# An mLSTM cell and a GELU layer on one core: 32-token products in the first chunk's values, and one batch of exponentials moved forward

## The chip, the cores and the metric

The kernel runs on one core of one Trainium2 chip. The metric is the time of one execution on the device in microseconds (us). A core has five engines with instruction streams of their own, each worked off in order: TensorE (PE in the profile; its weight loads are PEld), VectorE (DVE), ScalarE (ACT), GpSimd (POOL) and SyncE (SP), which here issues transfers. An instruction waits for others on semaphores.

## What is computed

The reference, cut to what matters. First a recurrent cell for each of 4 batches and 8 heads, over 768 tokens of width 40:

```python
for t in range(S):
    m_new = np.maximum(f_gate[:, :, t] + m, i_gate[:, :, t])
    f_stab = np.exp(f_gate[:, :, t] + m - m_new)
    i_stab = np.exp(i_gate[:, :, t] - m_new)
    m = m_new
    C = f_stab[:, :, None, None] * C + i_stab[:, :, None, None] * np.einsum('bhd,bhe->bhde', vt, kt)
    n = f_stab[:, :, None] * n + i_stab[:, :, None] * kt
    h_tilde = np.einsum('bhde,bhe->bhd', C, qt)
    denom = np.maximum(np.abs(np.einsum('bhd,bhd->bh', n, qt)[:, :, None]), 1.0)
    y[:, :, t] = 1.0 / (1.0 + np.exp(-o_gate[:, :, t])) * h_tilde / denom
```

Then the heads are laid side by side (3072 rows of 320) and go through two layers, `h = x @ w_in`, the exact GELU, `g @ w_out`, with a hidden width of 2048.

## The kernel before

The 768 tokens are six chunks of 128. Within a chunk the recurrence is written as products: scores of keys with queries, weighed by exponentials of the gates, times the values, and besides a contribution of the state that the chunks before have left. After the cell of a chunk its 512 rows (4 batches x 128 tokens) go through the two layers. The first chunk's up-projection takes part of its hidden rows as plain float32 products and part split in three parts that are added up; the later chunks take all of them in parts. In the input the layer weights are read as bit patterns and converted in pieces: ACT takes the two halves of a word apart (`conv_one`, lines 404 and 405, letter K of the order), DVE puts them together (`conv_two`, lines 416 and 419, letter J), and `fetch` (line 394) then loads a later piece into the buffer that has become free.

The order of the work is written out by hand, in strings of words that `play` (line 1019) works off one by one. A word is a letter and a batch number. `FRONT` (lines 26 to 31) holds the first chunk's cell in small letters, the second's in capitals, the conversions and the first chunk's two layers. All engines get their instructions in this order, and each keeps to it. The letters that the change and the prediction touch, for the second chunk and batch b:

- M: `mask`, line 474, on POOL: fills the upper triangle of the batch's tile W, which a transfer (`load_M`) has filled.
- W: `weights`, line 500, on ACT: eight exponentials, one per head, in place in W. For the first chunk (w) they are taken from PE's product pm.
- T: `turn`, lines 530 and 533: PE turns the batch's keys and queries into the bank pt, ACT copies them out as kT and qT.
- S: `scores`, lines 552 and 555: PE multiplies kT with qT, DVE multiplies the result into W.
- C: `carry`, lines 590 to 610: the state's part of the result and the state's update.
- V: `values`, line 656: PE multiplies W, now as the operand that is loaded, with the values, into the bank ph.
- Y and X: `finish` and `turn_y`, lines 685 to 718: the normalised output and its turned copy, whose high part x_hi ACT makes at line 718; DVE makes the rest at lines 727 and 728 (letter R).
- f2, f3: `first_pair`, lines 787 to 797: 36 products of the first chunk's up-projection in parts, and four GELUs on ACT.
- F: `first_down_steps`, line 888: the first chunk's down-projection; its last rows take split operands, whose middle part DVE makes at line 874.

In `values` a batch's eight heads go through the loop at line 655: in the first chunk each head's 128 tokens are two products of 64, in the second chunk four of 32. Each lands on its own partitions of ph:

```python
            for h in range(H):
                for r in halves if self.c == 0 else quarters:
                    nc.tensor.matmul(ph[r, h, :], Pm[:, h, r], vb[turn_of(n)][:, h, :], start=True, stop=True)
```

ACT keeps one set of function tables at a time. Where an exponential follows a GELU, or a GELU an exponential, the build places a load of the other set (ACT_TABLE_LOAD); copies and the conversions need none.

Of the kernel before, what the change touches and what calls it, by code (L numbers as in the profile page):

```python
# [25 lines left out]
FRONT = """  # L26
    O0 L0 k1 P0 E L1 L2 t0 P1 k7 K w0 g0 N s0 w1 O1 O3 D k4 t1 P2 w2 c0 v0 J y0 Q s1 L3 O2 K d w3 q t2 L4 P3 v1
    g1 c1 J y1 s2 K x0 t3 x1 v2 g2 O4 J B4 g3 c2 y2 s3 B5 K x2 K L5 J T0 K v3 A y3 M1 x3 c3 G0 M0 H O7 O6 O5 J
    J i5 u0 L6 u1 K W0 J W1 I4 A K S0 T1 C0 J i6 V0 i7 u2 G2 K U M2 L7 S1 J G1 K U i8 W2 J i9 C1 T2 K
    M3 f2 S2 V1 Y0 T3 J Y1 C2 e W3 K K K J S3 J C3 f3 K X0 J K R0 J K J V2 K Y2 J J K  # L30
    K V3 X1 J K r F J K (0 )0 F J K F K J F X2 G3 F J K F Y3 R1 J K F p + + + + J F J a10,2 b10,2 z10 a12 b12 F X3 z11 F a13,3 b13,3 z12 F z13 [1 F B8 z14 F B9 R2 z15 F R3 B10 B11 F a8 b8 a9 b9 F"""
CELL = "MWGVYXRKQDCSht"

# [23 lines left out]
def kernel(  # L57
# [95 lines left out]
    halves = (slice(0, R), slice(R, P))  # L153
    quarters = tuple(slice(R // 2 * n, R // 2 * (n + 1)) for n in range(4))
# [41 lines left out]
    def turn_of(n):  # L196

        return n % NLD if n < 2 * B else (n - 2 * B) % NQ
# [198 lines left out]
    def conv_one(i):  # L397

        if i < len(pieces):
            n = bits[i].shape[1]  # L400
            lo, hi = bits[i][:, :, 0], bits[i][:, :, 1]
            s = sig[i] = raw.tile([P, WP], F32, name="sig", tag="sig")[:, 0:n]
            p = pow2[i] = raw.tile([P, WP], U32, name="pow", tag="pow")[:, 0:n]
            nc.scalar.activation(out=s, in_=hi.bitcast(F32), func=AF.Copy, scale=2.0 ** -112)  # L404
            nc.scalar.activation(out=p, in_=lo, func=AF.Relu, scale=0.9 * 2.0 ** -29, bias=low_bits)
# [4 lines left out]
    def conv_two(i):  # L410

        if i < len(pieces):
            bits.pop(i)
            to = sig[i] if 4 < i < 10 else pieces[i][1]
            dst, s, p = to.bitcast(U32), (sig[i] if 4 < i < 10 else sig.pop(i)).bitcast(U32), pow2.pop(i)
            nc.vector.scalar_tensor_tensor(out=p, in0=s, scalar=3, in1=p, op0=OP.logical_shift_left, op1=OP.bitwise_or)  # L416
            if i >= 10:
                dst, s, p = in_pairs(dst), in_turns(s), in_turns(p)
            nc.vector.scalar_tensor_tensor(out=dst, in0=s, scalar=0x80000000, in1=p, op0=OP.bitwise_and, op1=OP.bitwise_or)  # L419
            if i != HELD:  # L420
                fetch(i + NB - (i > HELD))
# [8 lines left out]
    def unread(bank):  # L430
        for _ in range(idle[0]):
            nc.tensor.matmul(bank, ident, ident, start=True, stop=True, skip_group_check=True)
        idle[0] = 0
# [24 lines left out]
    class Cell:  # L458
# [190 lines left out]
        def values(self, b):  # L649
            n = self.c * B + b  # L650
            Pm = W.pop(n)
            ph = self.hs[b] = ps_h.tile([P, H, D1], F32, name="ph", tag="h")
            unread(ph.rearrange("p h d -> p (h d)")[:, 0:P])
            for h in range(H):
                for r in halves if self.c == 0 else quarters:
                    nc.tensor.matmul(ph[r, h, :], Pm[:, h, r], vb[turn_of(n)][:, h, :], start=True, stop=True)
            if self.c > 0:
                hs = self.hs[b] = self.far.pop(b)
                nc.vector.tensor_tensor(out=hs, in0=ph, in1=hs, op=OP.add)
# [172 lines left out]
    def first_up_steps(h):  # L832

        def step(k):
            ups.append((len(ups) + len(tags_next) % 2, (2 * k, 2 * k + 2, HT * h, HT * h + HT)))
            if len(ups) == 2:
                first_up()

        return [lambda k=k: step(k) for k in range(HF // 2)]
# [37 lines left out]
    def first_down_steps(g):  # L877
        po = []

        def row(n):  # L880

            if n == 0:
                po.extend(ps_mm.tile([P, DM], F32, name="po", tag="ab"[b // 2]) for b in range(B))
            xs, ws = ((g.row(n),), (w_row(n),)) if n not in first_parts_of else (first_parts_of[n], later.w_parts(n))
            steps = [(k, b) for k in range(len(xs)) for b in range(B)]
            for k, b in sorted(steps, key=lambda x: x[::-1]) if n == NF - 1 else steps:
                to, w = (po[b], ws[k]) if len(xs) == 1 else (in_pairs(po[b]), in_turns(ws[k]))
                nc.tensor.matmul(to, xs[k][:, b * L:(b + 1) * L], w, start=(n == 0 and k == 0),  # L888
                                 stop=(n == NF - 1 and k + 1 == len(xs)), skip_group_check=True)
                if n == NF - 1 and k + 1 == len(xs):  # L890
                    if b % 2 == 0:
                        o_sb = outp.tile([P, 2, DM], F32, name="o_sb", tag="o_sb")
                    nc.scalar.activation(out=o_sb[:, b % 2, :].rearrange("p (a i) -> p a i", a=2),
                                         in_=po[b].rearrange("p (i a) -> p a i", a=2), func=AF.Copy)
                    send(0, b, o_sb[:, b % 2, :])

        return [lambda n=n: row(n) for n in range(NF)]
# [128 lines left out]
    def in_turn(steps):  # L1026
        todo = list(steps)
        return lambda: todo.pop(0)() if todo else None
# [9 lines left out]
    def first_blocks():  # L1038
# [3 lines left out]
        for r in (32, 96):  # L1042
# [9 lines left out]
                 A=in_turn(first_up_steps(0)), U=in_turn(first_up_steps(1)), e=first_blocks, F=in_turn(first_down_steps(first_g)),  # L1052
                 K=in_turn(lambda i=i: conv_one(i) for i in n_pieces), H=products_begin,
                 J=in_turn(lambda i=i: conv_two(i) for i in n_pieces), Z=split_weight,
# [53 lines left out]
```

## Time and profile before

| | us |
|---|---|
| median of 3 runs | 438.06 |
| lowest and highest | 437.81, 439.68 |
| the profiled execution | 439.45 |
| its span in the profile | 437.7 |

The profile gives, for each engine, the busy time, and in a list by time each instruction or group of like instructions: start, length, engine, line, operation, the tile that is written and the tiles that are read, the shapes, the count, and in brackets how long the engine had been idle before and what ended that. The span runs from the first to the last instruction; the rest of an execution's time lies around it. Durations below come from this one execution.

### The profile page before, as it was taken

How to read it: one execution, taken by the hardware profiler on the slowest of the kernel's cores; microseconds unless marked ns; L12 is line 12 of the kernel's file. 1: busy time of each engine (PE TensorE's matmuls, PEld its weight loads, DVE VectorE, ACT ScalarE, POOL GpSimd, SP SyncE). 2: the span in 40 equal slices, each digit the busy share in tenths (PEclk: the TensorE clock that was granted, in tenths of full speed). 3: DMA queues.
4: the chain of work that ended last, by engine and by line, in shares of the span. 5: the costliest groups of instructions: out<-in, count | busy, mean ns of one | idle time of the engine just before them, and what ended most of it. 6: DMA issues, size and time to landing. Idle time of an engine off the chain costs nothing.

```text
span 437.7 us, 13034 instructions
## 1 busy us (share of the span) xinstructions
PE 429.5 (98%) x5344; PEld 376.6 (86%) x5344; DVE 295.6 (68%) x680; ACT 277.3 (63%) x595; POOL 50.0 (11%) x77
## 2 busy tenths in 40 slices
PE   9999999999999999999999999999999999999996
PEld 8778778877888898988898988898988889979986
DVE  7897777797888697737587737596746586533330
ACT  3989999965898985128776228795247715243441
POOL 3000212000530041030041030040010000000000
PEclk9999999999999999999999999999999999999999
DMA  7998996477791493563483564481561400010001
GB/s 153 198 211 228 196 247 164 124 197 197 210 184 56 88 191 63 108 172 63 65 179 69 107 165 69 94 157 32 108 157 18 61 1 1 18 45 1 1 1 60
DMA packets 162267, 48.81 MB, mean 112 GB/s; under 512 B 147776, under 2 KB 155232, under 8 KB 162208
## 3 DMA queue, kind: packets, MB, share of 16 engines
q1 hardware_dynamic: 161888, 47.65, 50.3%
q8 instruction: 42, 0.69, 0.7%
q10 hardware_dynamic: 320, 0.33, 0.2%
q14 instruction: 17, 0.14, 0.1%
HBM read 43.84 MB, written 9.37 MB: 122 GB/s over the span
## 4 chain that ended last, share of the span: by engine, by line
PE 73%; DVE 2%; ACT 2%; DMA 1%; issue 1%; ACTq 0%
PE po L991 31%; PE pu L966 24%; PE pu L977 7%; PE ps L568 3%; PE pf L621 2%; PE ph L674 1%; PE po L888 1%; PE po L674 1%; PE px L708 1%; DMA bits<-in_moe_w_out_dram 1%; PE pf L632 1%; ACT w_out_part L935 0%; DVE pow L416 0%; DVE w_out L419 0%; ACT sig L404 0%
## 5 line engine op out<-in xcount | busy, mean ns | idle before, releaser
L991 PE MATMUL po<-w_out_part,g_parts 128*128 128x320 f32 x960 | 140.7, 303 | 0.0
L991 PEld LDWEIGHTS po<-w_out_part,g_parts 128*128 128x128 f32 x960 | 131.6, 189 | 5.9 <-issue 4.6
L986 DVE TENSOR_TENSOR g_parts<-g_whole,g_parts 128x512 fp32r<-128x512 f32 x80 | 56.2, 702 | 57.8 <-ACT g_parts L985 55.7
L984 ACT ACTIVATE g_whole<-pu 128x512 f32<-128x512 f32 x80 | 47.2, 590 | 73.1 <-PE pu L977 62.6
L985 ACT ACTIVATE g_parts<-g_whole 128x512 fp32r<-128x512 f32 x80 | 50.5, 631 | 8.3 <-PE po L991 5.1
L474 POOL TENSOR_SCALAR_AFFINE_SELECT W<-W 128x1024 f32<-128x1024 f32 (+2 forms) x20 | 22.8, 1146 | 191.0 <-DMA W<-M_d 116.5
L500 ACT ACTIVATE W<-W,aT 128x128 f32<-128x128 f32 x128 | 38.7, 388 | 0.4 <-POOL W L474 0.2
L987 DVE CAST g_parts<-g_whole 128x512 fp32r<-128x512 f32 x80 | 36.3, 454 | 0.0
L699 ACT COPY far<-ob 128x128 f32<-128x128 f32 x16 | 4.6, 290 | 32.8 <-DVE ob L690 32.8
L966 PE MATMUL pu<-x_hi,w_in_hi 128*128 128x512 f32 x80 | 24.2, 384 | 0.0
L966 PE MATMUL pu<-x_hi,hi_first 128*128 128x512 f32 x80 | 23.9, 380 | 0.0
L966 PE MATMUL pu<-x_low,w_in 128*128 128x512 f32 x80 | 23.8, 379 | 0.0
L966 PE MATMUL pu<-x_rest,hi_first 128*128 128x512 f32 x80 | 23.8, 379 | 0.0
L966 PE MATMUL pu<-x_low,w_in_lo 128*128 128x512 f32 x80 | 23.8, 379 | 0.0
L966 PE MATMUL pu<-x_rest,w_in_hi 128*128 128x512 f32 x80 | 23.8, 379 | 0.0
L888 PE MATMUL po<-w_out,g 128*128 128x320 f32 x80 | 22.0, 432 | 0.0
L404 ACT ACTIVATE sig<-bits 128x320 f32<-128x320 f32 (+1 forms) x26 | 15.2, 585 | 10.6 <-issue 6.1
L574 DVE TENSOR_TENSOR W<-ps,W 128x256 f32<-128x256 f32 (+1 forms) x48 | 17.7, 413 | 4.2 <-PE ps L568 4.0
L888 PEld LDWEIGHTS po<-w_out,g 128*128 128x128 f32 x80 | 15.0, 190 | 5.9
L512 DVE STREAM_TRANSPOSE kT<-blocks 128x512 f32<-128x512 f32 x16 | 11.3, 709 | 12.0 <-DMA blocks<-kq_d 11.8
L639 DVE TENSOR_TENSOR far<-pf,gT 128x164 f32<-128x164 f32 x32 | 8.4, 319 | 14.7 <-PE pf L632 11.4
L1015 ACT ACTIVATE o_sb<-po 128x320 f32<-128x320 f32 x20 | 7.5, 442 | 16.7 <-PE po L991 16.7
(196 smaller groups left out, 788.3 us busy)
## 6 DMA issues: line engine op xcount, KB each, us to landing
W<-M_d SPq DMA_DIRECT2D x16, 512.0 KB, 6.6
bits<-in_moe_w_in_dram SPq DMA_DIRECT2D x20, 256.0 KB, 4.7
bits<-in_moe_w_out_dram SPq DMA_DIRECT2D x16, 320.0 KB, 4.8
blocks<-kq_d SPq DMA_DIRECT2D x32, 128.0 KB, 3.5
ob<-in_o_gate_dram SPq DMA_DIRECT2D x24, 160.0 KB, 4.3
out_dram<-o_sb SPq DMA_DIRECT2D x36, 80.0 KB, 2.0
wide<-M_d SPq DMA_DIRECT2D x4, 512.0 KB, 4.8
kq_d<-in_k_dram SPq DMA_DIRECT2D x6, 320.0 KB, 4.8
```

Source lines behind the costliest of these rows:

```text
L404: nc.scalar.activation(out=s, in_=hi.bitcast(F32), func=AF.Copy, scale=2.0 ** -112)
L474: nc.gpsimd.affine_select(out=x, in_=x, compare_op=OP.is_ge, fill=1.0e30, base=base, pattern=[[0, H], [1, x.shape[2]]], channel_multiplier=-1)
L500: nc.scalar.activation(out=W[n][:, h, :], in_=src, func=AF.Exp, scale=-1.0, bias=aT[:, self.c, r:r + 1])
L574: nc.vector.tensor_tensor(out=w[r, :, t], in0=ps[i][hip][r, :, t], in1=w[r, :, t], op=OP.mult)
L888: nc.tensor.matmul(to, xs[k][:, b * L:(b + 1) * L], w, start=(n == 0 and k == 0), stop=(n == NF - 1 and k + 1 == len(xs)), skip_group_chec ...
L966: nc.tensor.matmul(in_pairs(pus[i][e]), w3(at[k])[n][:, e, i * P:(i + 1) * P], in_turns(x3[n][:, k, :]), start=(n == 0 and k == 0), stop=F ...
L977: nc.tensor.matmul(in_pairs(pus[i][e]), w3(r)[n][h, p % 2, i * P:(i + 1) * P], in_turns(x3[n][h, NX, :]), start=False, stop=(n == 2), skip ...
L984: nc.scalar.activation(out=whole, in_=self.pus[n // 4][n % 4 // 2][n % 2], func=AF.Gelu)
L985: nc.scalar.activation(out=hi, in_=whole, func=AF.Copy, scale=PART)
L986: nc.vector.tensor_tensor(out=rest, in0=whole, in1=hi, op=OP.subtract)
L987: nc.vector.tensor_copy(out=low, in_=whole)
L991: nc.tensor.matmul(in_pairs(self.po[t]), x[:, t * L:(t + 1) * L], in_turns(w), start=(n == 0 and k == 0), stop=(n == NF - 1 and k == 2), s ...
```

## The change

Two things. In `values` the loop takes quarters of 32 tokens in the first chunk too. And in the written order the second chunk's fourth mask, M3, stands ahead of its old place by some words, and its fourth batch of exponentials, W3, directly behind T2 (the third batch's kT and qT) and so ahead of a conversion (K), the pair f2 and T3. In the order of the instructions this moves nothing on POOL, DVE and SP; on PE only the form of the values' products differs; on ACT the eight exponentials move up past one conversion, four GELUs and the two copies of T3, and two table loads are no longer placed.

```diff
-    J i5 u0 L6 u1 K W0 J W1 I4 A K S0 T1 C0 J i6 V0 i7 u2 G2 K U M2 L7 S1 J G1 K U i8 W2 J i9 C1 T2 K
-    M3 f2 S2 V1 Y0 T3 J Y1 C2 e W3 K K K J S3 J C3 f3 K X0 J K R0 J K J V2 K Y2 J J K
+    J i5 u0 L6 u1 K W0 J W1 I4 A K S0 T1 C0 J i6 V0 i7 u2 G2 K U M2 L7 S1 J G1 M3 K U i8 W2 J i9 C1 T2 W3 K
+    f2 S2 V1 Y0 T3 J Y1 C2 e K K K J S3 J C3 f3 K X0 J K R0 J K J V2 K Y2 J J K
...
-                for r in halves if self.c == 0 else quarters:
+                for r in quarters:
```

## The prediction

> **What bounds the kernel now.** I read the page first, then the waits of TensorE (PE), then the stretches ahead of the change, then the order of time on each engine.
>
> ```profile
> PE 429.5 (98%) x5344; PEld 376.6 (86%) x5344; DVE 295.6 (68%) x680; ACT 277.3 (63%) x595; POOL 50.0 (11%) x77
> ```
>
> PE is busy 98% of the span of 437.7 us, so nearly every microsecond that PE loses or gains is a microsecond of the kernel, unless a wait further on takes it up. The next view is the list of waits of PE alone between 33 and 126 us; its columns are the total, the count and the longest, in us.
>
> ```profile
> PE po L888 <- DVE g_part L874: 0.7, 2, 0.4
> PE ps L552 <- ACT qT L533: 0.4, 1, 0.4
> PE ph L656 <- DVE W L555: 0.3, 1, 0.3
> ```
>
> Three waits, 1.4 us in all, are everything that PE loses there. So a saving ahead of the waits at lines 656 and 552 only makes these longer, if the engines that end them keep their time; and a loss behind them can be taken up only by the 0.7 us at line 888. Which engine keeps that time is told by two rows of the stretches (their length, then the busy time of PE, PEld, DVE, ACT and POOL, then the granted clock, the share of the transfer engines, GB/s):
>
> ```profile
> 16.00:34.00 18.00, 16.59 (x266) 14.23 (x268) 15.03 (x41) 14.99 (x44) 0.00 (x0) 1.00 1.06 217
> 45.00:68.97 23.97, 23.30 (x260) 19.27 (x257) 17.25 (x28) 23.73 (x52) 6.43 (x6) 1.00 1.07 242
> ```
>
> From 45 to 68.97 us ScalarE (ACT) is busy 23.73 of 23.97 us: it has more to do than PE and has no hole. In the first chunk, 16 to 34 us, nobody is full (PE waits 1.41 us, ACT 3.01 us), but the transfer engines are (share 1.06). Now the order of time on ACT, on which the whole sum rests:
>
> ```profile
> 33.81 0.69 ACT L404 ACTIVATE sig<-bits 128x512 f32<-128x512 f32 x1 [1.60 <-DMA bits<-in_moe_w_in_dram]
> ...
> 55.66 0.62 ACT L533 COPY qT<-pt 128x512 f32<-128x512 f32 x1
> ...
> 68.49 0.57 ACT L533 COPY qT<-pt 128x512 f32<-128x512 f32 x1
> 68.97 0.62 ACT L404 ACTIVATE sig<-bits 128x320 f32<-128x320 f32 x1
> ...
> 70.19 1.28 ACT L797 ACT_TABLE_LOAD   x1
> 71.48 2.07 ACT L797 ACTIVATE g<-pu 128x512 f32<-128x512 f32 x4
> 73.52 0.59 ACT L533 COPY kT<-pt 128x512 f32<-128x512 f32 x1
> 74.12 0.59 ACT L533 COPY qT<-pt 128x512 f32<-128x512 f32 x1
> 74.72 1.28 ACT L500 ACT_TABLE_LOAD   x1
> 76.02 2.44 ACT L500 ACTIVATE W<-W,aT 128x128 f32<-128x128 f32 x8
> 78.37 0.57 ACT L404 ACTIVATE sig<-bits 128x320 f32<-128x320 f32 x1
> ...
> 81.96 1.28 ACT L797 ACT_TABLE_LOAD   x1
> 83.81 2.06 ACT L797 ACTIVATE g<-pu 128x512 f32<-128x512 f32 x4 [0.56 <-PE pu L793]
> 85.73 0.55 ACT L404 ACTIVATE sig<-bits 128x320 f32<-128x320 f32 x1
> ...
> 86.64 0.51 ACT L718 ACTIVATE x_hi<-px 128x384 fp32r<-128x384 f32 x1
> ```
>
> The reader is to see that ACT's dense stretch starts on a transfer at 33.81, and that the copies of kT and qT of the fourth batch (73.52, 74.12) end at 74.71. PE needs them here:
>
> ```profile
> 74.50 0.77 PE L595 MATMUL pf<-state,qT 128*64 128x82 f32 x16
> 75.20 1.16 PE L552 MATMUL ps<-qT,kT 64*128 64x128 f32 x16
> 76.29 0.67 PE L590 MATMUL pf<-vw,qk 128*64 128x41 f32 x16
> ...
> 77.48 1.99 PE L787 MATMUL pu<-first_x_hi,hi_first 128*128 128x512 f32 x8
> ...
> 84.35 0.44 PE L708 MATMUL px<-ident,ob 128*128 128x128 f32 x2
> ```
>
> The scores of the fourth batch (75.20) follow the products before them at once: qT was ready 75.20 - 74.71 = 0.49 us early. That is all the slack there is.
>
> **The exponentials moved.** The fourth batch's eight exponentials (line 500, 76.02) go from behind the fourth batch's kT and qT to behind the third's, that is to 68.97, ahead of a conversion (lines 404, 405), the load of the GELU table and four GELUs. Nothing new is issued; on GpSimd, VectorE and SyncE's queue the order stays. Two table loads fall away: at 68.97 the exponential's table is still in place, so the load at 74.72 goes, and with no exponential between the two groups of GELUs the load at 81.96 goes too, 2 x 1.28 = 2.56 us of ACT. The exponentials wait for the fourth batch's mask:
>
> ```profile
> 64.56 1.55 POOL L474 TENSOR_SCALAR_AFFINE_SELECT W<-W 128x1024 f32<-128x1024 f32 x1 [1.31 <-PE pt L530]
> ```
>
> It ends at 66.11, 2.86 us before 68.97: no wait is added there. But now the ready time of qT is put together anew, from the same rows, each step from its start to the start of the next: exponentials 78.37 - 76.02 = 2.35; conversion 70.19 - 68.97 = 1.22; table load 71.48 - 70.19 = 1.29; four GELUs 73.52 - 71.48 = 2.04; kT 68.97 - 68.49 = 0.48 (that spacing stands for kT as for qT, since both copies have their operand by then); qT 0.57. So qT ends at 68.97 + 2.35 + 1.22 + 1.29 + 2.04 + 0.48 + 0.57 = 76.92. The step from the end of that copy to PE's start is in a row quoted below: the second batch's copy ended at 55.66 + 0.62 = 56.28, its scores started at 56.34, 0.06 later. Scores then start at 76.98 and not at 75.20: **PE loses 1.78 us**. Behind the waiting scores stand, on PE, the fourth batch's carry (76.29) and the 36 products of the last up-projection pair (77.48 to 84.35); all start 1.78 later. Their banks are free by then (the four GELUs end 2.35 later, at 75.90, before 77.48 + 1.78).
>
> What the loads saved is worth: nothing. The load at 74.72 lay behind the copies that PE waits for. The load at 81.96 ended at 83.24, and the GELUs behind it waited until 83.81 for PE; PE now comes later. The exponentials themselves were in no hurry where they stood, since their reader on VectorE (DVE) came at 80.56, after they had ended at 78.46:
>
> ```profile
> 80.56 1.28 DVE L555 TENSOR_TENSOR W<-ps,W 128x512 f32<-128x512 f32 x2
> ```
>
> What is late next: the GELUs go from 83.81 to 85.59, behind them on ACT the conversion at 85.73 and the x_hi copy at 86.64, and from there the chain of work that ended last goes on without a hole:
>
> ```profile
> 87.18 0.56 DVE x_rest L727
> ...
> 113.88 6.24 PE po L888 x44
> ```
>
> Between these two rows it runs through DVE, ACT and one transfer of the output weights, and comes back to PE at 113.88, which is one of the two waits at line 888. So the chain that ends that wait begins with the very GELUs that are 1.78 late. Both PE (dense from 84.35) and the chain slip by the same amount, so I let the 0.7 us take up nothing. Full cover would be worth 0.7.
>
> **The values of the first chunk.** Each of four batches is 16 products of 64 columns, now 32 of 32 columns; the trace shows two records per product. It also shows the new form, in the second chunk:
>
> ```profile
> 18.58 1.11 PE L656 MATMUL ph<-vb,W 128*64 128x41 f32 x32
> 19.62 0.37 PE L276 MATMUL pg<-ident,ew 32*128 32x32 f32 x3
> ...
> 56.34 1.16 PE L552 MATMUL ps<-qT,kT 64*128 64x128 f32 x16 [0.36 <-ACT qT L533]
> ...
> 85.59 0.81 PE L656 MATMUL ph<-v,W 128*32 128x41 f32 x64
> 86.33 0.44 PE L708 MATMUL px<-ident,ob 128*128 128x128 f32 x2
> ```
>
> Old form: 19.62 - 18.58 = 1.04 us to the next work. New: 86.33 - 85.59 = 0.74. So 0.30 saved a batch, at most 1.2 us in all. The Trainium skill, TensorE: Matmul & The Clock Gate, section "Wait — 56ns, not 53.3ns?", speaks against the edit: starts never come closer than about 25 ns, and by that 64 records would take 1.6 us, 0.56 more than now. This trace differs: 0.74 us for 64 records is 12 ns each, since four column groups take turns, and the measurement decides.
>
> What it is worth at the end: the first of the four batches starts at 18.58 and all stand on PE ahead of the scores at 56.34. PE comes 1.2 us earlier to what follows and waits there, at line 656 for DVE and at 56.34 for ACT (0.36 now). ACT's time at 56.34 goes back without a hole to 33.81, where it waited 1.60 us for a transfer of input weights. The queue that issued it:
>
> ```profile
> 28.61 1.95 SPq L394 DMA_DIRECT2D bits<-in_moe_w_in_dram x4
> ```
>
> By the code that load's buffer is fresh, so PE need not release it; the loads ahead of it need only early work of the first batch. I therefore take 0 for this edit. The bounds: 0 if the transfers keep their time; if the queue does wait for PE, the two batches ahead of 28.61 give up to 0.6; all four cannot give more than 1.2 by PE alone.
>
> **The sum.** +1.78 (scores late) + 0 (loads, exponentials) + 0 (values) = +1.78 us. For the profiled execution that is 437.7 + 1.78 = 439.5 of span and 439.45 + 1.78 = 441.2 of time. That execution was 1.39 above the median of the runs, 438.06; on the median the forecast is 438.06 + 1.78 = **439.8 us**. A measurement of this kernel can tell about 0.5%, or 2.2 us, from no change, so this is a small loss that would count as the same.
>
> **The rivals.**
> (a) The early gain is handed on in part: ACT's dense stretch starts 0.5 sooner, 439.3. For it: the saved time does lie ahead of 33.81, and the wait view puts some of the queue's waits down to PE there. Against it: transfer share 1.06.
> (b) The waits at line 888 take up the 0.7: 439.1. For it: the conversions at 78.37 start about 1.5 us earlier (they follow the start of qT, 76.92 - 0.57 = 76.35, by 0.48), so some weights are fetched sooner. Against it: the chain above.
> (c) Faster. ACT has 3.01 us of waits between 16 and 34. If the shorter values let more than 1.78 of them go, no scores wait is left and the kernel gains; with all 3.01 gone it ends at 438.06 + 1.78 - 3.01 = 436.8. Against it: 1.60 of the 3.01 is the transfer at 33.81, and PE saves only 1.2.
> (d) Slower: PE's clock falls in the new hole. The hole lies between small products, and the start of the kernel shows what a slow clock costs:
>
> ```profile
> 3.82 2.08 PE L250 MATMUL cold<-w_out 128*128 128x128 f32 x8
> ...
> 9.24 1.73 PE L250 MATMUL cold<-w_out 128*128 128x128 f32 x14
> ```
>
> 260 ns each at 3.82 against 124 at 9.24, the granted clock notwithstanding, so about twice as slow; slow work lasted from about 1.1 to 5.8 us, 4.8 us. The same after the hole would lose half of that, 2.4 us, off the products from 77.48: 439.8 + 2.4 = 442.2. It decides if a hole of 1.78 us is enough; the holes of up to 0.4 us above were not. The same page of the Trainium skill, section "What's actually happening", gives about 3.4 us idle as the point where the clock drops, which no row here shows; by that the hole is too short, and where it did drop, half of 3.4, 1.7 us, would be lost.
>
> **How the numbers follow.** The forecast has 0.55, (a) 0.15, (b) 0.08, (c) 0.07, (d) 0.15. The forecast, (a) and (b) lie between 439.1 and 439.8; with 0.7 either side for the spread of the runs (437.81 to 439.68) that is 438.4 to 440.5. Half of (d), with a shorter slow stretch, brings the top to 441.5; left out are (c) and the rest of (d). Over 440.25 lies (d) and about a fifth of the forecast: slower 0.27. Under 435.9 lies only an end beyond (c)'s: faster 0.03. The same 0.70.
>
> **What would show it right or wrong.** A wait of PE for ACT's qT at the fourth batch's scores, near 1.7 us, with the exponentials at about 69.0, one table load between 65 and 100 us behind them, and GELUs at about 85.6: right. If that wait is absent, the step of ACT's rows was wrong. If ACT's conversion near 33.8 comes sooner, (a) or (c). If the two waits at line 888 are gone while the chain before them kept its time, (b). If the 36 products take more than 6.9 us, (d). If the values of the first chunk still take about 1.0 us a batch, the edit doesn't do what it says, at no cost to the sum.

## The result and the profile after

| | before | after |
|---|---|---|
| median of 20 executions each, us | 438.4 | 439.8 |
| lowest and highest | 437.38, 440.1 | 438.78, 441.87 |
| the profiled execution, its span | 439.45, 437.7 | 440.12, 438.3 |

The ratio is 1.0029, 95% interval 1.0019 to 1.0039: on 438.4 us a loss of 1.3 us, 0.8 to 1.7. The forecast was 439.8, from 438.06, the median of the first three executions, plus 1.78. That it meets the measured time to the tenth is luck: with 20 executions the kernel before stands at 438.4, 0.34 higher, and the loss is smaller than 1.78 by about as much.

The page of the kernel after, its line of busy times:

```profile
PE 428.4 (98%) x5472; PEld 375.2 (86%) x5472; DVE 296.1 (68%) x680; ACT 273.7 (62%) x593; POOL 50.4 (11%) x77
```

PE's busy time fell by 1.1 us and ACT's by 3.6, with two instructions fewer on ACT (the table loads), and yet the span grew by 0.6: busy time saved is not time gained. PE's waits of the kernel after, 33 to 126 us, tell where it went:

```profile
PE ps L552 <- ACT qT L533: 1.8, 2, 1.4
PE po L888 <- DVE g_part L874: 0.8, 2, 0.4
PE ph L656 <- DVE W L555: 0.2, 1, 0.2
```

The wait for qT was 0.4 us in one place; now it is 1.8 in two, with a new one of 1.4. Its place, in PE's order of time of the kernel after:

```profile
18.46 0.82 PE L656 MATMUL ph<-vb,W 128*32 128x41 f32 x64
19.21 0.37 PE L276 MATMUL pg<-ident,ew 32*128 32x32 f32 x3
...
34.29 3.72 PE L818 MATMUL pu<-first_x,w_in 128*128 128x256 f32 x16
...
55.44 1.16 PE L552 MATMUL ps<-qT,kT 64*128 64x128 f32 x16 [0.35 <-ACT qT L533]
...
75.78 1.16 PE L552 MATMUL ps<-qT,kT 64*128 64x128 f32 x16 [1.40 <-ACT qT L533]
...
78.06 1.99 PE L787 MATMUL pu<-first_x_hi,hi_first 128*128 128x512 f32 x8
...
84.93 0.44 PE L708 MATMUL px<-ident,ob 128*128 128x128 f32 x2
```

The fourth batch's scores (75.78) are what waits. From 78.06 to 84.93 the 36 products take 6.87 us, as before (77.48 to 84.35). The values of a batch take 19.21 - 18.46 = 0.75 us. And on ACT, after:

```profile
68.07 2.45 ACT L500 ACTIVATE W<-W,aT 128x128 f32<-128x128 f32 x8
70.41 0.48 ACT L404 ACTIVATE sig<-bits 128x320 f32<-128x320 f32 x1
...
71.40 1.28 ACT L797 ACT_TABLE_LOAD   x1
72.69 2.06 ACT L797 ACTIVATE g<-pu 128x512 f32<-128x512 f32 x4
74.62 0.62 ACT L533 COPY kT<-pt 128x512 f32<-128x512 f32 x1
75.08 0.65 ACT L533 COPY qT<-pt 128x512 f32<-128x512 f32 x1
...
79.74 0.63 ACT L404 ACTIVATE sig<-bits 128x320 f32<-128x320 f32 x1 [2.28 <-issue]
...
84.39 2.06 ACT L797 ACTIVATE g<-pu 128x512 f32<-128x512 f32 x4 [3.42 <-PE pu L793]
```

The order is the one foretold: exponentials, conversion, one load, GELUs, then the fourth batch's kT and qT. The second group of GELUs waits 3.42 us for PE, where it waited 0.56, and a conversion at 79.74 starts after 2.28 us of idle time that was not there before. What ACT no longer does between the copies and these GELUs, the exponentials and two loads, has turned into idle time.

**Where executions differ.** The profiled execution of before lies 1.05 us above its median (439.45 against 438.4), the one of after 0.3 (440.12 against 439.8), so single starts can't be subtracted across kernels. Two points make them comparable: the first GELUs of the first chunk (line 828), and the second batch's scores. First the kernel before, PE's products that feed those GELUs, then ACT's GELUs:

```profile
35.00 3.72 PE L818 MATMUL pu<-first_x,w_in 128*128 128x256 f32 x16
```

```profile
40.39 1.08 ACT L828 ACTIVATE g<-pu 128x512 f32<-128x512 f32 x2
```

And after, on ACT, the conversion at the start of the dense stretch and the same GELUs:

```profile
32.89 0.69 ACT L404 ACTIVATE sig<-bits 128x512 f32<-128x512 f32 x1 [1.10 <-DMA bits<-in_moe_w_in_dram]
...
39.50 1.09 ACT L828 ACTIVATE g<-pu 128x512 f32<-128x512 f32 x2
```

From the GELUs to the second batch's scores it is 56.34 - 40.39 = 15.95 us before and 55.44 - 39.50 = 15.94 after: the same. From there to the fourth batch's scores it is 75.20 - 56.34 = **18.86 before and 75.78 - 55.44 = 20.34 after: the move costs 1.48 us**. Ahead of the GELUs the profiled execution of after is 0.89 us sooner (39.50 against 40.39), which leaves the 0.6 by which the span grew; from the fourth batch's scores to the end it is 362.5 us in both. That last stretch differs among executions too: it is 361.5 with the move alone and 361.6 with the values alone, two of the runs below. So the stage between the scores is read from the profiles, and what a kernel is worth as a whole from the times.

### The profile page after: what moved, and what is told of

Read it like the earlier page. It is cut to its first block, busy times and chain, and to the rows that moved or that the text cites. A ratio compares the mean times of both kernels' runs of the same rounds, so it can differ in the third digit from the quotient of the medians.

```text
span 438.3 us, 13289 instructions
## 1 busy us (share of the span) xinstructions
PE 428.4 (98%) x5472; PEld 375.2 (86%) x5472; DVE 296.1 (68%) x680; ACT 273.7 (62%) x593; POOL 50.4 (11%) x77
## 4 chain that ended last, share of the span: by engine, by line
PE 73%; DVE 1%; issue 1%; SPq 1%; DMA 1%; ACT 1%; ACTq 0%
PE po L991 31%; PE pu L966 24%; PE pu L977 7%; PE ps L568 3%; PE pf L621 2%; PE po L888 2%; PE ph L674 1%; PE po L674 1%; PE px L708 1%; PE pf L632 1%; DMA bits<-in_moe_w_out_dram 1%; SPq L289 1%; SPq L182 0%; ACT sig L404 0%; DVE pow L416 0%
## 5 line engine op out<-in xcount | busy, mean ns | idle before, releaser
L416 DVE SCALAR_TENSOR_TENSOR pow<-sig,pow 128x320 uint32<-128x320 uint32 (+1 forms) x26 | 15.5, 594 | 4.7 <-ACT pow L405 4.7
```

## The experiments

The theory: the move delays the fourth batch's qT, and that is the whole loss; the values' saving is worth nothing. The rivals: the values matter too; the loads matter; PE's clock falls in the hole. In the kernels that make products twice or add some, the added ones have no reader or rewrite the same values, so the results are the same.

**The two halves apart.** The move alone (in the kernel after):

```diff
-                for r in quarters:
+                for r in halves if self.c == 0 else quarters:
```

> The exponentials are moved as in the change; the first chunk's values stay products of 64 tokens. Theory: the whole change is the late qT of the fourth batch, so the scores wait for ACT about 1.7 us and the kernel is 1.5 to 1.8 us slower than before, no less than the full change. Rival 1 (the 32-token products hand on a gain to ACT's dense stretch): 1.8 us slower, and the full change less than that by about 0.5. Rival 2 (the loss does not come from the scores' wait): about as the full change, 1.3, with no wait above 1 us at the fourth batch's scores.

The values alone (in the kernel before):

```diff
-                for r in halves if self.c == 0 else quarters:
+                for r in quarters:
```

> Only the first chunk's values become products of 32 tokens; the exponentials stay. Theory: 0 us against before (within 0.2), the values take 0.75 us a batch in place of 1.04, and PE's waits at the second batch's scores and values grow by what is saved. Rival 1: 0.4 to 0.9 us faster, with ACT's conversion near 33.8 us sooner by as much and everything behind it too.

Measured: the move alone 1.0020 (1.0005 to 1.0035), +0.9 us, 0.2 to 1.5; the values alone 0.9982 (0.9966 to 0.9998), -0.8 us, -1.5 to -0.1. The move is the loss, though 0.9 lies under the 1.5 to 1.8 expected and the interval only just reaches 1.5. The values do gain a little by themselves, against my 0. They leave the stage of the scores alone: with the values alone it takes 74.24 - 55.38 = 18.86 us from the second batch's scores to the fourth's, as before. The move alone, PE's and then ACT's order of time:

```profile
34.75 3.72 PE L818 MATMUL pu<-first_x,w_in 128*128 128x256 f32 x16
...
55.50 1.16 PE L552 MATMUL ps<-qT,kT 64*128 64x128 f32 x16 [0.33 <-ACT qT L533]
...
75.86 1.16 PE L552 MATMUL ps<-qT,kT 64*128 64x128 f32 x16 [1.42 <-ACT qT L533]
```

```profile
32.39 0.69 ACT L404 ACTIVATE sig<-bits 128x512 f32<-128x512 f32 x1 [0.44 <-DVE y_rest L699]
...
39.56 1.09 ACT L828 ACTIVATE g<-pu 128x512 f32<-128x512 f32 x2 [0.59 <-PE pu L824]
```

Second to fourth scores: 75.86 - 55.50 = 20.36, as in the kernel after. But here the weights landed early, the conversion ran at 32.39, and then the GELUs waited 0.59 us **for PE**. That is a join that the prediction had missed: the GELUs start at the later of the conversion's start + 6.6 us (39.50 - 32.89, after) and the start of PE's products + 4.81 (39.56 - 34.75, here). In the profiled execution of before these are 33.81 + 6.6 = 40.4 and 35.00 + 4.81 = 39.81, so PE was only 0.6 us from being the bound. With the values alone, on PE, then ACT:

```profile
34.25 3.72 PE L818 MATMUL pu<-first_x,w_in 128*128 128x256 f32 x16
```

```profile
32.84 0.69 ACT L404 ACTIVATE sig<-bits 128x512 f32<-128x512 f32 x1 [1.09 <-DMA bits<-in_moe_w_in_dram]
```

PE's side is at 34.25 + 4.81 = 39.06, 0.75 sooner than before, and the transfer's side (32.84 + 6.6 = 39.4) decides again. Part of the 0.75 is a difference between executions: with the move alone, which has the long products, PE's products for the GELUs start at 34.75, in the kernel after at 34.29, only 0.46 sooner. So the shorter values help in the executions in which the weights land early, and there by about 0.5 to 0.75 us. How many executions those are is not known; in the six profiles with the short products once and the fetches in their old order the GELUs start between 38.99 and 40.14 and none waits for PE. Of the 1.2 us about 0.7 comes back as longer waits of PE: between 24 and 36 us the two below stand at 0.7 and 0.5 in the kernel after, where before had 0.3 and 0.2:

```profile
PE pf L590 <- DVE vw L539: 0.7, 1, 0.7
PE px L708 <- DVE y_rest L699: 0.5, 1, 0.5
```

**Less ahead of qT.** The conversion goes behind the fourth batch's kT and qT (in the kernel after; dots within a row of code stand for words left out here):

```diff
-    ... C1 T2 W3 K
-    f2 S2 V1 Y0 T3 J ...
+    ... C1 T2 W3
+    f2 S2 V1 Y0 T3 K J ...
```

> The full change, but the conversion that stood between the moved exponentials and the GELU table's load goes behind the fourth batch's copies of kT and qT. Theory: qT is ready sooner by what that conversion took on ACT (1.0 to 1.2 us), the scores' wait shrinks from 1.4 to 0.2-0.4 us, and the kernel is 1.0 to 1.2 us faster than the full change, 0.1 to 0.3 slower than before. Rival 2: as the full change, 1.3 slower than before.

Measured: 0.9996 (0.9978 to 1.0013), -0.2 us, -1.0 to 0.6: no loss left to see. Its PE:

```profile
55.20 1.16 PE L552 MATMUL ps<-qT,kT 64*128 64x128 f32 x16 [0.34 <-ACT qT L533]
...
74.67 1.16 PE L552 MATMUL ps<-qT,kT 64*128 64x128 f32 x16 [0.54 <-ACT qT L533]
```

Second to fourth scores 19.47: 0.87 of the 1.48 is back, about the conversion's 0.99 (70.41 to 71.40 after). The length of ACT's queue ahead of qT is what counts.

**More ahead of qT.** The exponentials behind the GELUs of the pair f2, so that both loads come back (in the kernel after):

```diff
-    ... C1 T2 W3 K
-    f2 S2 ...
+    ... C1 T2 K
+    f2 W3 S2 ...
```

> The full change, but the moved exponentials stand behind the four GELUs of the first pair, still ahead of the fourth batch's copies of kT and qT, so that both table loads are back. Theory: qT is late by 2.35 us of exponentials and 1.29 us of table load, less 0.49 of slack, so the scores start 3.2 us later than before and the kernel is 2.7 to 3.2 us slower than before. Rival 2 (something else than the scores' wait costs the time): 1.3 us or less, since the conversion and the GELUs are again where they were.

Measured: 1.0079 (1.0052 to 1.0106), +3.5 us, 2.3 to 4.7. PE's order of time, then its stretches (length; busy PE, PEld, DVE, ACT, POOL; granted clock, transfer share, GB/s):

```profile
54.96 1.16 PE L552 MATMUL ps<-qT,kT 64*128 64x128 f32 x16 [0.35 <-ACT qT L533]
...
76.97 1.73 PE L552 MATMUL ps<-qT,kT 64*128 64x128 f32 x16 [3.08 <-ACT qT L533]
...
80.78 1.99 PE L787 MATMUL pu<-first_x_hi,hi_first 128*128 128x512 f32 x8
```

```profile
76.00:78.00 2.00, 1.03 (x12) 1.03 (x14) 1.88 (x7) 2.00 (x5) 0.00 (x0) 0.85 0.00 0
78.00:80.00 2.00, 2.00 (x32) 1.78 (x30) 1.97 (x5) 1.40 (x4) 0.00 (x0) 0.50 0.53 106
80.00:82.00 2.00, 2.00 (x20) 1.69 (x17) 1.95 (x6) 1.51 (x2) 0.00 (x0) 0.80 1.21 243
```

Second to fourth scores 22.01, 3.15 more than before (3.2 expected). And, not expected, behind the 3.08 us hole the granted clock falls to 0.50: from the scores to the pair's products it is 80.78 - 76.97 = 3.81 us against 78.06 - 75.78 = 2.28 after, 1.53 lost. Rival (d)'s mechanism exists; the change's own hole of 1.40 us does not set it off. The clocks of the single executions bear it out: five of the six have a mean granted clock of 0.994 to 0.996 and take 442.84 to 443.81 us, the sixth has 1.000 and takes 440.76. So even here the fall does not come every time.

**The hole filled.** Products that nothing reads, ahead of the third batch's carry and so of the waiting scores: nine (I9), then four (I4), in the kernel just shown. The trace has two records for each, 18 and 8.

```diff
-    f2 W3 S2 V1 Y0 T3 J Y1 C2 e ...
+    f2 W3 S2 V1 Y0 T3 J Y1 I9 C2 e ...
```

> The kernel with the exponentials behind the first pair's GELUs, and nine products of the identity that nobody reads ahead of the third batch's carry, so that PE's hole of 3.1 us before the fourth batch's scores is filled to about 0.6. Theory: the granted clock stays at 1.00 behind it, the scores and the carry behind them take 2.3 us again and not 3.8, and the kernel is about 1.5 us faster than the same without the filling, about 2 us slower than before. Rival (the slow clock costs nothing that is not lost anyway, or falls for another reason): as without the filling, 3.5 us slower than before.

> The kernel with the exponentials behind the third batch's GELUs (hole of 3.08 us ahead of the fourth batch's scores, granted clock 0.50 behind it), with 8 products that nothing reads ahead of the hole, about 0.97 us by the 18 products in 2.17 us of the run with the hole filled: a hole of about 2.1 us is left, between the 1.40 us at which the clock held and the 3.08 us at which it fell. If the deciding point lies above 2.1 us: clock 1.00 in the windows behind, scores and carry 2.3 us, 442.0 us. If it lies below: clock 0.50 behind the scores, scores and carry 3.8 us, 443.5 us.

With nine, on PE:

```profile
78.11 1.16 PE L552 MATMUL ps<-qT,kT 64*128 64x128 f32 x16 [1.03 <-ACT qT L533]
...
80.39 1.99 PE L787 MATMUL pu<-first_x_hi,hi_first 128*128 128x512 f32 x8
```

With four, on PE, then the stretch behind the scores, with a granted clock of 0.56:

```profile
77.58 1.53 PE L552 MATMUL ps<-qT,kT 64*128 64x128 f32 x16 [2.19 <-ACT qT L533]
...
81.18 2.20 PE L787 MATMUL pu<-first_x_hi,hi_first 128*128 128x512 f32 x8
```

```profile
78.00:80.00 2.00, 2.00 (x32) 1.77 (x30) 1.92 (x6) 1.41 (x4) 0.00 (x0) 0.56 0.24 37
```

A hole of 1.03 leaves 2.28 us from scores to pair, the full clock; 2.19 gives 3.60 and the fall. So in these profiles, at this place, the deciding point lies between 1.40 and 2.19. As whole kernels they gave 1.0077 (1.0047 to 1.0106), +3.4 us, and 1.0106 (1.0078 to 1.0134), +4.7: the one with nine is the faster by 1.3 us, as the stage has it, but not by more than the intervals hold, and against the unfilled one (1.0079) the time shows no gain. The 2 us that the theory expected for nine were missed; 3.4 is the rival's figure. What the filling does to the clock is plain, 0.999 to 1.000 in all six executions, and in the profile the stage gains its 1.53; that the kernel gains is not shown.

**What the early part is worth.** The transfer of layer weights on which ACT's conversion waits goes ahead of the loads of the second chunk's first queries and keys (P3 ahead of L4), in the kernel before, then with the values of 32 tokens too:

```diff
-    ... t2 L4 P3 v1
+    ... t2 P3 L4 v1
```

> The kernel before with one edit: the transfer of input weights that ACT's conversion near 33 us waits for (the word P3) is issued ahead of the loads of the next chunk's first queries and keys (L4), about 3 us sooner. Theory (ACT's dense stretch begins with this transfer and PE's times from 56 us on follow it): ACT's conversion near 33 comes about 1 us sooner, the second batch's scores near 56 too, and the kernel is 0.4 to 1.0 us faster than before. Rival (the stretch is set by later transfers or by PE): within 0.3 us of before.

> The transfer issued sooner as in the run beside it, and the first chunk's values as products of 32 tokens; the exponentials where they were before. If the 32-token products work through ACT's start near 33 us, the two edits overlap and this is 0.5 to 1.2 us faster than before, hardly more than the better of the two alone. If the products work by another way, the gains add: 1.2 to 1.8 us faster. If neither is worth anything: within 0.3 us.

Measured: 1.0011 (0.9981 to 1.0041), +0.5 us, and 0.9983 (0.9964 to 1.0002), -0.7. The first missed the gain of 0.4 to 1.0 that was expected; the second fits an overlap of the two edits and not their sum. (The first's interval is wide: three of its executions, at a mean granted clock of 0.991 to 0.996, take 442.0 to 443.8 us; why is not known.) ACT's GELUs, in the first kernel and then in the second:

```profile
39.94 1.08 ACT L828 ACTIVATE g<-pu 128x512 f32<-128x512 f32 x2 [1.37 <-PE pu L824]
```

```profile
39.21 1.09 ACT L828 ACTIVATE g<-pu 128x512 f32<-128x512 f32 x2 [0.67 <-PE pu L824]
```

In both the conversion no longer waits for the transfer, and in both PE ends the GELUs' wait, 0.73 us sooner with the short products. Of this 0.19 is a wait that only the first of the two profiles has, for the keys that now come behind the weights:

```profile
33.07 0.63 PE L530 MATMUL pt<-ident,wide 128*128 128x128 f32 x4 [0.19 <-DMA wide<-in_k_dram]
```

Neither edit is worth more than the join lets through, and the second adds nothing that can be seen to the values alone.

Then the dose the other way, all 128 tokens in one product:

```diff
-                for r in halves if self.c == 0 else quarters:
+                for r in (slice(0, P),) if self.c == 0 else quarters:
```

> The kernel before with the first chunk's values as products of all 128 tokens: 16 instructions a batch in place of 32, so the dose goes the other way and with fewer instructions, where the run with every product twice had more. Estimate of the price: TensorE's turns at L530 in the kernel before, eight products with a 128x128 operand in 1.06 us, 0.13 us each, so 16 are 2.1 us a batch in place of 1.04, +4.2 us over the four. Theory A (the values lie beside waits: ScalarE's dense stretch begins at a transfer, and TensorE is idle 1.6 us between 15 and 34 us): the first 1.6 us are taken up, +2.6 us or less, 441 us. Theory B (TensorE's time there is on the path whole): +4.2 us, 442.6 us; then the 1.2 us that products of 32 tokens save are worth about 1 us too. Theory C on the run with every product twice (its 4.4 us stop was for instructions that had not arrived): no wait for nothing shown here, since there are fewer of them.

Measured: 1.0040 (1.0025 to 1.0056), +1.8 us, 1.1 to 2.5. On PE, then on ACT:

```profile
18.83 1.98 PE L656 MATMUL ph<-vb,W 128*128 128x41 f32 x16
20.74 0.37 PE L276 MATMUL pg<-ident,ew 32*128 32x32 f32 x3
...
37.41 3.70 PE L818 MATMUL pu<-first_x,w_in 128*128 128x256 f32 x16
```

```profile
42.21 1.09 ACT L828 ACTIVATE g<-pu 128x512 f32<-128x512 f32 x2 [1.68 <-PE pu L824]
```

A batch takes 1.91 us, 0.87 more than the 1.04 of before, 3.5 over four; PE's products for the GELUs start 2.41 later (waits took up the rest), the GELUs 1.82 later (the 0.6 of slack went first), and the kernel is 1.8 slower. That these two agree is partly luck, since the profiled execution of before was a late one: against the move alone, with its GELUs at 39.56, it is 2.65. Either way less than the 3.5 is passed on, so theory A holds and theory B does not, and the join gives the GELUs' start here too (37.41 + 4.81 = 42.22).

**Products of 32 made twice.** An attempt at the same dose by repetition, in all four batches, and later in the first two only:

```diff
-                for r in halves if self.c == 0 else quarters:
+                for r in quarters * 2 if self.c == 0 else quarters:
```

```diff
-                for r in halves if self.c == 0 else quarters:
+                for r in quarters * (2 if n < 2 else 1) if self.c == 0 else quarters:
```

> The kernel before with the first chunk's values taken as products of 32 tokens and each of them made twice over, so that a batch's values take about 1.5 us of PE in place of 1.04, 0.46 more (1.8 us in all, opposite in sign to the change's saving). Theory (the values lie beside waits): within 0.4 us of before. Rival (their length is passed on in full): 1.8 us slower, and then the change's saving is worth up to 1.2.

> The kernel before with products of 32 tokens in the first chunk, made twice in the batches 0 and 1 and once in the batches 2 and 3 (results the same): 128 instructions more than with each made once, half of what the run with all four twice had. Theory C (the stop of 4.4 us in the run with all twice was for instructions that had not arrived, since PE used them up faster than they came while the DMA engines were busy): the stop gets shorter by the instructions saved, 0 to 2 us, later than the second batch, and the granted clock holds, 438 to 441 us. Rival (it is the repeated product that stops the engine, in whichever batch): a stop inside batch 0 or 1. Without any stop: TensorE's time is 1.5 us more than with products of 32 made once, and 0.3 us more than in the kernel before, 438 to 439 us.

Measured: 1.0230 (1.0194 to 1.0266), +10 us, 8.5 to 11.7, and 1.0090 (1.0064 to 1.0116), +4.0. Both expectations missed. The profiled executions, each the quickest of its six, have the second batch's scores 8.1 and 2.3 us later than before; the rest of the 10 and 4.0 is not traced. All four batches twice, on PE, and the row of the queue that brings instructions:

```profile
28.09 1.04 PE L552 MATMUL ps<-qT,kT 64*128 64x128 f32 x13 [1.01 <-issue]
...
30.80 1.16 PE L656 MATMUL ph<-vb,W 128*32 128x41 f32 x99
36.39 0.77 PE L656 MATMUL ph<-vb,W 128*32 128x41 f32 x29 [4.44 <-issue]
```

```profile
q8 instruction: 45, 0.74, 0.7%
```

PE stops in the midst of a group of like products, for 1.01 us after 3 of 16 records of scores and for 4.44 us after 99 of 128 of values, and waits for nothing that the profile shows. Between the stops it issued 13 records of scores, 6 that turn outputs, 8 that turn keys and queries, and the 99 of values: 126 records, each with its load of an operand: 252 instructions. The queue is PE's: over the kernels with 5344, 5472, 5600 and 5728 records it has 42, 43, 44 and 45 pieces, one more for each 128 records, that is for each 256 instructions. Its 0.74 MB, spread over PE's 2 x 5728 instructions, are 65 bytes each, and a piece of 16.4 KB holds about 254 of them. So by the count both stops lie at the seams of pieces, and the reading that fits is that the next instructions had not arrived; no row shows a piece arrive. With the first two batches alone the first stop stays, at the very same product, and the second is gone:

```profile
27.97 1.04 PE L552 MATMUL ps<-qT,kT 64*128 64x128 f32 x13 [1.13 <-issue]
```

The rival, that the repeated product itself stops the engine, does not fit: the same groups of 128 records ran through at 24.66 with no stop. That the piece was late because the transfer engines are full there (share 1.04 between 15 and 34 us in the kernel before, by its stretches) is an argument, not shown.

## Why the prediction was right

1. **PE is the bound, and its wait for qT sets the loss**: right. The wait appeared at the scores named, 1.40 us.
2. **The sum over ACT's rows**: right in every step, a little too long. From the exponentials' start to qT's end I had 7.95 us; after it is 75.73 - 68.07 = 7.66, the conversion 0.99 in place of 1.22 and the GELUs 1.93 in place of 2.04 making most of it. That 0.3 is why the stage lost 1.48 and not 1.78; the measured loss of 0.8 to 1.7 holds the one, not the other. The size of this term was a little off, and the exact hit of 439.8 owes itself to a base that was too low by about the same.
3. **The loads are worth nothing**: right by the rows. ACT's 2.56 us went into its idle time of 2.28 and 3.42 us behind the copies. No run takes the loads away without the move.
4. **The values are worth nothing**: right in its mechanism, the join with the transfer, and incomplete. I took ACT's dense stretch as bound by the transfer alone; PE's side was 0.6 us behind it, and in executions in which the weights land early it decides. Alone the edit gained 0.8 (0.1 to 1.5). How much it gave beside the move stays open: the whole change against the move alone, 1.0029 against 1.0020, shows no gain, within about 0.8 us.
5. **The waits at line 888 take up nothing**: right in the two profiles, 0.8 us after against 0.7. But these waits differ by execution (0.4 with the move alone, none with the values alone), so rival (b) was not seen, which is less than ruled out.
6. **The clock holds in the new hole**: right; the 36 products took 6.87 us. The deciding point was nearer than I thought: 2.19 us sufficed at this place, and the loss was 1.5 us, less than the 2.4 I had given it. That figure came from the lengths of products at the kernel's start, where the granted clock reads 1.00 all the same.
7. **Rival (a)**, an early gain handed on in part, happens, as the values alone show; beside the move its 0.5 us and the 0.3 by which my own term was too large can't be told apart by the times.

The best version is the values alone, 0.9982 (0.9966 to 0.9998) of before: the move is left out.

## What to carry to other kernels

When an instruction is moved up on an engine that feeds the bound, add up everything that now stands ahead of the next result the bound waits for; table loads saved elsewhere on that engine do not pay for it. Look for joins: where two engines end a wait within half a microsecond of each other, a saving on the one is worth only the difference. And a hole on TensorE costs more than its length when the clock falls behind it: here that came after holes of 1.13 to 3.08 us, not every time, and after the one of 3.08 it cost 1.5 us more.

## What the runs showed of the hardware

- **The clock** fell after holes of 3.08, 2.19 and 1.13 us (the last with products made twice in two batches) and held after 1.42, 1.40 and 1.03. So the length of one hole alone does not decide. The slow time was the same after each of the three: the clock's shortfall behind the 3.08 us hole is (0.15 + 0.50 + 0.20) x 2 us = 1.70 us, at half clock 3.4 us. With the 1.13 us hole:

```profile
28.00:30.00 2.00, 2.00 (x19) 1.88 (x20) 1.06 (x2) 0.67 (x2) 0.00 (x0) 0.79 1.00 154
30.00:32.00 2.00, 2.00 (x14) 1.67 (x13) 1.97 (x5) 1.30 (x3) 0.00 (x0) 0.50 0.99 304
32.00:34.00 2.00, 2.00 (x87) 1.90 (x88) 0.87 (x5) 1.59 (x6) 0.00 (x0) 0.86 1.14 323
```

  (0.21 + 0.50 + 0.14) x 2 / 0.5 = 3.4 us again, and with 0.56 and 0.59 behind the 2.19 us hole (0.44 + 0.41) x 2 / 0.5 = 3.4. In and behind the 4.44 us hole, with 0.81, three times 0.50 and 0.99 from 34 to 44 us, it is 6.8, twice as much. If the clock goes from 1.00 to 0.50 in one step, the slow time began 0.4, 0.7 and 1.2 us after the holes of 3.08, 2.19 and 1.13 had ended (an estimate from the same windows). The Trainium skill, TensorE: Matmul & The Clock Gate, section "What's actually happening", says that activity is judged in windows of about 3.4 us that run freely; the 3.4 us of slow clock agree, and a hole's place in the window would explain why 1.13 fell and 1.42 held, which no run here tests. Its rule that it takes about one idle window did not hold: 2.19 us was enough, and the 1.13 us hole too.
- **Instructions arrive in pieces.** The Trainium skill, Runtime: NRT & Kernel Launch, section "Instruction fetch mechanics", gives blocks of 256 instructions, fetched ahead and mostly hidden. The size agrees (252 between two stops); that it is hidden did not hold for batches of 128 records of 32 tokens, each in 1.4 us: 4.44 us of stop, if the reading above is right. In the kernel after, with 64 records a batch, no such wait shows between 10 and 60 us.
